# Other assumed DMA durations in the build-time planner of a two-layer transformer kernel, and the program order that follows from them

## The chip, the cores and the metric

One core of a Trainium2 chip runs the whole kernel. The metric is the device time of one execution in microseconds (us). The kernel uses all five instruction streams of the core: TensorE (PE, with its weight loads shown as PEld), VectorE (DVE), ScalarE (ACT), GpSimd (POOL) and SyncE (SP), which here only issues DMA transfers.

## The reference, cut to what matters

Two identical layers over a sequence of 2048 tokens with 512 features; attention has 32 heads of 16 features, the feed-forward part 1792 hidden features. All arrays are bf16.

```python
def A(x, wqkv, wo):                      # attention
    q, k, v = heads(x @ wqkv)            # 32 heads, Dh = 16
    p = softmax(q @ k^T * Dh ** -0.5)    # 2048 x 2048 per head
    return heads_back(p @ v) @ wo
def B(x, w1, b1, w2, b2):                # feed-forward
    return gelu(x @ w1 + b1) @ w2 + b2
for layer in range(2):
    x = x + A(layernorm(x), wqkv, wo)
    x = x + B(layernorm(x), w1, b1, w2, b2)
```

## The kernel before

**Tiling.** The 2048 queries of a layer are cut into four segments of 512 (the very last one into two of 256). A pass takes one segment and four heads (eight passes a segment, line 1109), and walks over 16 key tiles of 128. A cell is one head, one key tile and 512 queries: its scores are one matmul (L1244), which three cells share side by side, and their exponentials fill 512 columns of PSUM for each cell. Most cells go to ACT, two or three to an instruction (L1601, `0.065 + 0.4267 * n` in the planner's units); the others go to DVE and POOL, which make the exponential by integer arithmetic on the bits (L1396 from PSUM, then L1473 on POOL and L1478 on DVE). The product with V (L1665) gathers a pass in one PSUM bank, and `norm` (L805) divides by the sum.

**What runs beneath it.** Attention of one segment runs while PE also does the rest of the layer for the segment before it: the output projection `wo` (L861), a layer norm, the first feed-forward matmul `hpair` (L948), gelu on ACT (L982), the second matmul `ytile` (L1001), the next layer norm and the next layer's projections (L777). All their matmuls are recorded at L556, in steps of eight matmuls, four of which stand side by side in the PE array.

**Weights.** Feed-forward and projection weights don't stay on the core. `wloads` (L891) streams them as pieces of 256 KB into a ring of four buffers `wr`, each load issued by SP at L933 when the matmuls that used the buffer before are done. Each tile of `ytile` alone takes seven such pieces. For the last half segment four pieces go to a part of `kt` instead (`wlate`, L937); all four write under the same keys (`over`), so each of them waits for the one before it to land.

**Layer norm.** DVE takes the statistics, POOL scales a 128-token tile into one of two buffers `xln` (L689), and SP issues a DMA transpose of it into `xf`, `xp` or `kt` (L693). Only the first four tiles and the last two are transposed by PE instead (L700).

**Who sets the order.** Nothing is written in order by hand. Each part above is a Python generator that yields operations (`_Op`, L186) with an engine, an assumed duration `cost`, and, for a DMA, an assumed `tail` from the end of its issue to its landing. `_Sched.run` (L362) keeps a clock for each engine, picks the operation that can start first by its own arithmetic (with priorities among those that are ready), and appends it to that engine's program. The end that others wait for is set in one line:

```python
self.end[ev] = start + cost + op.tail + LATENCY[e]          # L420
```

The semaphore waits come from the true data dependencies (`_Prog`, L84), so the order is free of races whatever is assumed; what the assumed durations change is only where each instruction stands in its engine's program. Each engine runs its program strictly in order. Where PE would be free for a while by the plan, `fill` (L340) puts matmuls without a use into its program (L1232). Feed-forward steps are also held back to set fractions of the attention's progress (`when`, L1038, with the tables `HB`, `HS`, `YB`, `YS`, `PACE`).

The lines that the change touches: `LATENCY` (L212), the moves of `x` between HBM and the core (`xmove`, L621), the DMA transpose (L693), the weight load (L933) and the store of the output (L1034).

Of the kernel before, what the change touches and what calls it, by code (L numbers as in the profile page):

```python
# [28 lines left out]
XT = 8  # L29
# [179 lines left out]

OWN = 0.022  # L210
HEAD = 0.14
LATENCY = {"pe": 0.219, "act": 0.21, "dve": 0.139, "pool": 0.153328, "sp": 0.1}  # L212
OVERLAP = 0.083
ROUND = 1.02

# [1 line left out]
class _Sched:  # L217
# [122 lines left out]
    def fill(self, start, nxt):  # L340
        while self.filler and self.mode:
# [17 lines left out]
            self.clock["pe"] = now + into + MM + cold  # L359
            self.end[ev] = self.clock["pe"] + LATENCY["pe"]  # L360

    def run(self):  # L362
        while True:
# [55 lines left out]
            self.clock[e] = start + cost  # L419
            self.end[ev] = start + cost + op.tail + LATENCY[e]  # L420
            for x in op.after:
# [4 lines left out]
                self.clock[e] = at + MM  # L426
                self.end[ev] = at + MM + LATENCY[e]
            if e == "dve" and op.port:
# [117 lines left out]
class _Plan:  # L546
# [72 lines left out]
        yield ("give", "loaded")  # L619

    def xmove(self, c, src, dst, sem, reads, writes):  # L621
        yield _Op("sp", 0.42, lambda e: e.dma_start(dst, src), reads=reads, writes=writes, sem=sem, by=16, tail=3.7)

    def xfeed(self, h):
        keys = ["X.%d" % (t % XT) for t in range(4 * h, 4 * h + 4)]
# [58 lines left out]
    def ln_tile(self, c, t, dst, dkeys, quick):  # L684
        T = self.T
        ph = self.phase[t // 4]
        x = yield ("acq", "xln")
        eng, cost = ("dve", 0.4) if quick else ("pool", 0.77)
        yield _Op(eng, cost, lambda e: e.tensor_scalar(  # L689
            T["XLN"][:, x, :], T["X"][:, t % XT, :], T["RSTD"][:, t:t + 1], T["NMR"][:, t:t + 1], op0=ALU.mult, op1=ALU.add),  # L690
            reads=["X.%d" % (t % XT), "RSTD.%d" % c, "NMR.%d" % c], writes=["XLN.%d" % x])
        if not quick:
            yield _Op("sp", 1.2, lambda e: e.dma_start(dst(t), T["XLN"][:, x, :], transpose=True),  # L693
                      reads=["XLN.%d" % x], writes=dkeys(t), sem="dtr%d" % x, by=16, tail=1.35)
            yield ("rel", "xln", x)
            yield ("give", ("lnt", t, ph))
            return
        b = yield ("acq", "misc")
        tb = self.bank(b).bitcast(BF16)
        fns = [lambda e, dc=dc: e.transpose(tb[:, dc * 128:(dc + 1) * 128], T["XLN"][:, x, dc * 128:(dc + 1) * 128],  # L700
                                            T["IDENT"][:, :]) for dc in range(NDC)]
        yield _Op("pe", 4 * TR, fns, reads=["XLN.%d" % x, "IDENT"], writes=["B.%d" % b], prio=0.8)
        yield ("rel", "xln", x)
        t3 = tb[:, 0:512].rearrange("p (c q) -> p c q", c=NDC)
        if ph == 0 or t % 2 == 0:
            yield _Op("act", DV, lambda e: e.copy(dst(t), t3), reads=["B.%d" % b], writes=dkeys(t))
        else:
            yield _Op("dve", DV, lambda e: e.tensor_copy(dst(t), t3), reads=["B.%d" % b], writes=dkeys(t))
        yield ("rel", "misc", b)
        yield ("give", ("lnt", t, ph))  # L710
# [219 lines left out]

    def wload(self, piece, src, n, uses, w, over):
        dst = self.T["WR"][w].rearrange("p (c f) -> p c f", c=n)
        yield _Op("sp", 0.37, lambda e: e.dma_start(dst, src), writes=["WR.%d" % w] + over, sem="dwr%d" % w, by=16, tail=2.48)  # L933
        self.wleft[piece] = uses
        yield ("give", ("w",) + piece, w)

# [64 lines left out]
    def ytile(self, l, seg, t):  # L1001
        T = self.T
        tail = l == NL - 1 and seg[0] == self.NQ - 1
        last = NFC // 2 - 1
        for p in range(1 if tail else NFC // 2):
            yield ("need", ("g", l, seg, p))
        b = None if tail else (yield ("need", ("w", l, seg, "2", (t, 0))))
        b = yield ("acq", "misc")
        pb = self.bank(b)
        q = slice((t % 4) * 128, (t % 4) * 128 + 128)  # L1010
        for p in range(NFC // 2):
            yield ("need", ("g", l, seg, p))
            if tail and p < last:
                yield ("need", ("w2", p // 2))
                wk, ws = "W2.%d" % (p // 2), [T["Q"][:, f % 4, 512 * (f // 4):512 * (f // 4) + 512] for f in (2 * p, 2 * p + 1)]
            else:
                piece = (NL - 1, self.segs[NL - 1][-1], "2", last) if tail else (l, seg, "2", (t, p))
                w = yield ("need", ("w",) + piece)
                wk, ws = "WR.%d" % w, [T["WR"][w][:, 512 * j:512 * j + 512] for j in range(2)]
            fns = []  # L1020
            for j in range(2):
                fns += self.quads(pb, T["G"][:, 2 * p + j, q], ws[j], p + j == 0, False)
            if p == last:
                fns += self.quads(pb, T["ONES1"][:, :], T["B2row"][:, :], False, True)
            yield _Op("pe", len(fns) // 4 * MM, fns, reads=[wk, "ONES1", "B2row"] + ["G.%d.%d" % (f, t % 4) for f in (2 * p, 2 * p + 1)],
                      writes=["B.%d" % b], prio=MID if p else FPRIO, mode="P")
            if not tail or p == last:
                yield from self.wdone(piece, w)
        yield _Op("dve", DV, lambda e: e.tensor_tensor(out=T["X"][:, t % XT, :], in0=T["X"][:, t % XT, :], in1=pb, op=ALU.add),
                  reads=["B.%d" % b, "X.%d" % (t % XT)], writes=["X.%d" % (t % XT)])  # L1030
        yield ("rel", "misc", b)
        yield ("give", ("xready", t, 2 * l + 2))
        if l == NL - 1:
            yield _Op("sp", 0.42, lambda e: e.dma_start(self.hbm["out"][:, t, :], T["X"][:, t % XT, :]), reads=["X.%d" % (t % XT)],  # L1034
                      writes=["OUT.%d" % t], sem="dout", by=16, tail=2.0)
            yield ("give", ("xout", t))

# [735 lines left out]
```

## Time and profile before

| | |
|---|---|
| median of three runs | 1532.86 us (1531.32 to 1536.05) |
| the profiled execution | 1531.3 us |
| its span, first to last instruction | 1529.5 us |
| busy: PE, DVE, ACT, POOL | 1441.2, 1335.0, 1477.3, 821.9 us |
| mean granted TensorE clock | 0.999 |
| DMA traffic | 103.40 MB, 68 GB/s on the mean |

The span leaves out 1.8 us of the profiled execution's own time (1531.3 less 1529.5). The profiled execution lies 1.6 us below the median. "Idle before" in the views below is the time in which an engine stood still ahead of an instruction, with what ended it; matmuls overlap each other, so their durations can't be added.

### The profile page before, as it was taken

The numbers are of one execution on the slowest core, as the hardware profiler recorded it, in microseconds if no ns is written. First come the engines' busy times: TensorE is split into PE (matmuls) and PEld (weight loads), VectorE is DVE, ScalarE is ACT, GpSimd is POOL, SyncE is SP. The second block draws the span as 40 slices with busy tenths as digits, with TensorE's granted clock in tenths as the row PEclk, the third lists the DMA queues.
The fourth block names the chain that finished last, engine by engine and source line by source line (L and its number), as shares of the span: only waits on it lengthen the run. The fifth ranks groups of instructions, "written<-read, shape, count | busy, mean of one in ns | idle before, by whom it ended". The sixth has DMA issues, their size and how long they took to land.

```text
span 1529.5 us, 46372 instructions
## 1 busy us (share of the span) xinstructions
PE 1441.2 (94%) x20257; PEld 441.6 (29%) x20257; DVE 1335.0 (87%) x2259; ACT 1477.3 (97%) x1369; POOL 821.9 (54%) x785
## 2 busy tenths in 40 slices
PE   8998899999999999999999999899999999999998
PEld 3222222222222222222222222222222222334345
DVE  6568889989998999978799778899989989999994
ACT  7999999999999999999999999999999999999995
POOL 5435546655564755545465455567555646464550
PEclk9999999999999999999999999999999999999999
DMA  5100001052111521126121441001143105311523
GB/s 155 41 2 1 2 12 40 29 174 77 48 31 53 144 83 36 43 64 166 50 56 38 130 133 29 1 2 36 37 151 93 43 23 170 109 36 33 167 69 98
DMA packets 145046, 103.40 MB, mean 68 GB/s; under 512 B 37069, under 2 KB 143822, under 8 KB 144846
## 3 DMA queue, kind: packets, MB, share of 16 engines
q1 hardware_dynamic: 144846, 100.44, 23.2%
q8 instruction: 162, 2.65, 0.7%
q14 instruction: 38, 0.31, 0.1%
HBM read 88.61 MB, written 4.19 MB: 61 GB/s over the span
## 4 chain that ended last, share of the span: by engine, by line
ACT 40%; PE 39%; DVE 14%; DMA 5%; POOL 1%; issue 1%; SPq 0%; DVEq 0%; ACTq 0%; POOLq 0%
ACT pt L1601 32%; PE ps L556 13%; PE ps L1665 13%; PE ps L1244 12%; DVE du L1396 6%; DVE du L1478 4%; DMA wr<-in_B_w_dram 2%; ACT kt L1601 2%; ACT q L1601 2%; ACT g L997 2%; DVE g L976 1%; ACT v L1601 1%; POOL xln L689 1%; DMA kt<-in_B_w_dram 1%; DMA xp<-xln 1%
## 5 line engine op out<-in xcount | busy, mean ns | idle before, releaser
L1601 ACT ACTIVATE pt<-ps 128x1024 bf16<-128x1024 f32 (+1 forms) x1112 | 1198.2, 1218 | 19.1 <-PE ps L1244 13.3
L1473 POOL TENSOR_SCALAR du<-du 128x1024 uint16<-128x1024 uint16 (+1 forms) x479 | 562.2, 1175 | 495.6 <-DVE du L1396 481.2
L1396 DVE TENSOR_SCALAR du<-ps 128x512 uint16<-128x512 f32 x956 | 634.9, 680 | 93.5 <-PE ps L1244 88.6
L1244 PE MATMUL ps<-qp,kt 32*128 32x512 bf16 x4096 | 530.0, 384 | 37.3 <-ACT pt L1601 20.7
L1665 PE MATMUL ps<-pt,v 128*17 128x512 bf16 (+1 forms) x2876 | 407.3, 360 | 11.4 <-ACT pt L1601 6.3
L1665 PE MATMUL ps<-du,vc 128*17 128x512 bf16 (+1 forms) x3228 | 384.3, 357 | 3.5 <-ACT pt L1601 1.8
L1478 DVE TENSOR_SCALAR du<-du 128x2048 uint16<-128x2048 uint16 (+1 forms) x479 | 351.4, 743 | 10.7 <-POOL du L1473 10.6
L1244 PEld LDWEIGHTS ps<-qp,kt 32*128 32x128 bf16 x4096 | 137.2, 91 | 581.6 <-ACT pt L1601 214.1
L1665 PE MATMUL ps<-du,v 128*17 128x512 bf16 (+1 forms) x1076 | 178.7, 358 | 10.3 <-ACT pt L1601 3.3
L1673 PE MATMUL ps<-vc,zero 128*17 128x512 bf16 x919 | 182.5, 381 | 0.0
L556 PE MATMUL ps<-xf,wr 128*32 128x512 bf16 (+1 forms) x1888 | 129.5, 364 | 4.2 <-DMA xf<-xln 2.0
L1665 PEld LDWEIGHTS ps<-pt,v 128*17 128x17 bf16 x2876 | 99.2, 88 | 108.0 <-issue 65.2
L1665 PEld LDWEIGHTS ps<-du,vc 128*17 128x17 bf16 x3228 | 100.2, 89 | 89.5 <-issue 54.8
L556 PE MATMUL ps<-wr,g 128*32 128x512 bf16 x1600 | 117.6, 384 | 7.6 <-DMA wr<-in_B_w_dram 6.4
L1192 POOL TENSOR_SCALAR qp<-q,mask 128x512 bf16<-128x512 bf16 (+1 forms) x91 | 71.1, 781 | 76.6 <-PE ps L1244 69.9
L1601 ACT ACTIVATE kt<-ps 128x1536 bf16<-128x1536 f32 (+1 forms) x77 | 98.9, 1294 | 2.9 <-PE ps L1244 1.2
L976 DVE TENSOR_SCALAR g<-ps,hb1t 128x512 bf16<-128x512 f32 (+1 forms) x112 | 78.4, 703 | 6.0 <-PE ps L556 5.4
L1473 POOL TENSOR_SCALAR kt<-kt 128x1024 uint16<-128x1024 uint16 (+1 forms) x46 | 53.4, 1161 | 46.9 <-DVE kt L1396 46.8
L1601 ACT ACTIVATE v<-ps 128x1024 bf16<-128x1024 f32 (+1 forms) x69 | 73.9, 1139 | 2.0 <-PE ps L1244 1.2
L1396 DVE TENSOR_SCALAR kt<-ps 128x512 uint16<-128x512 f32 x91 | 62.0, 681 | 7.3 <-PE ps L1244 5.6
L1665 PE MATMUL ps<-kt,v 128*17 128x512 bf16 (+1 forms) x309 | 67.5, 365 | 0.3 <-ACT pt L1601 0.2
L1665 PEld LDWEIGHTS ps<-du,v 128*17 128x17 bf16 x1076 | 45.1, 88 | 63.3 <-issue 25.7
(90 smaller groups left out, 1234.0 us busy)
## 6 DMA issues: line engine op xcount, KB each, us to landing
wr<-in_B_w_dram SPq DMA_DIRECT2D x256, 256.0 KB, 2.9
wr<-in_A_wqkv_dram SPq DMA_DIRECT2D x24, 256.0 KB, 3.0
wr<-in_A_wo_dram SPq DMA_DIRECT2D x18, 256.0 KB, 3.6
x<-in_A_x_dram SPq DMA_DIRECT2D x7, 512.0 KB, 4.1
kept<-x SPq DMA_DIRECT2D x4, 512.0 KB, 2.9
x<-kept SPq DMA_DIRECT2D x4, 512.0 KB, 3.9
out_dram<-x SPq DMA_DIRECT2D x16, 128.0 KB, 2.4
g<-in_A_wqkv_dram SPq DMA_DIRECT2D x3, 512.0 KB, 5.1
```

The costliest lines, as they stand in the source:

```text
L556: return [lambda e, a=a: e.matmul(out[32 * a:32 * a + 32, :], lhsT=lhsT[:, 32 * a:32 * a + 32], rhs=rhs, start=start, stop=stop, tile_posi ...
L689: yield _Op(eng, cost, lambda e: e.tensor_scalar(T["XLN"][:, x, :], T["X"][:, t % XT, :], T["RSTD"][:, t:t + 1], T["NMR"][:, t:t + 1], op0 ...
L976: yield _Op("dve", 0.21 + n / 966, lambda e, fc=fc, pb=pb: e.tensor_scalar(T["G"][:, fc, q], pb, T["HB1T"][:, fc:fc + 1], None, op0=ALU.ad ...
L997: lambda e, g=g: e.activation(out=g, in_=g, func=ACT.Gelu_apprx_tanh), reads=gk, writes=gk, prio=2)
L1192: yield _Op("pool", 0.27 + 0.42 * w / 512, lambda e, s=s, q=q, i=i, t=t, w=w: e.tensor_scalar(T["QP"][:, s, w * i:w * i + w], q, T["MASK"] ...
L1244: return (lambda e: e.matmul(o, lhsT=lhsT, rhs=rhs, start=True, stop=True, tile_position=(32 * a, 0)), ["K%d.%d.%d" % (l, gb, kt // 4), "Q ...
L1396: yield _Op("dve", 0.682, lambda e: e.tensor_scalar(u, self.bank(b), E_SCALE, E_BIAS, op0=ALU.mult, op1=ALU.add), reads=["B.%d" % b], writ ...
L1473: one = _Op("pool", 0.15 + 0.45 * n, lambda e, a=a, b=b: e.tensor_scalar(b, a, float(SHIFT), 1.0, op0=ALU.add, op1=ALU.mult), reads=key[0] ...
L1478: two = _Op("dve", 0.152 + 0.266 * n, lambda e: e.tensor_scalar(U[:, 2:4, 0:n, :], U[:, 0:2, 0:n, :], 2 * SHIFT, None, op0=ALU.add), reads ...
L1601: yield _Op("act", 0.065 + 0.4267 * n, lambda e, src=src, dst=dst: e.activation(out=dst, in_=src, func=ACT.Exp, scale=0.25), reads=["B.%d" ...
L1665: op.fns.append(lambda e, o=o, lhsT=q[0][0][m], rhs=q[0][1][:, n * m:n * m + n], a=a, st=st, sp=sp: e.matmul(o, lhsT=lhsT, rhs=rhs, start= ...
L1673: op.fns.append(lambda e, o=self.bank(b)[32 * a:32 * a + 17, :], rhs=rhs, a=a, st=not begun[a], sp=end: e.matmul(o, lhsT=T["ZERO"][:, 0:17 ...
```

## The change

Five entries of the planner's table take other values; no operation, buffer, dependency or priority is edited. "Issue" is the time that the plan takes on SP, "tail" the time from there to landing; with SP's 0.1 of `LATENCY` the three add up to the assumed time from issue to use.

| operation | issue + tail before | after |
|---|---|---|
| `xmove` (512 KB) | 0.42 + 3.7 | 1.5 + 4.0 |
| DMA transpose | 1.2 + 1.35 | 0.3 + 3.5 |
| weight load (256 KB) | 0.37 + 2.48 | 1.5 + 2.5 |
| output store | 0.42 + 2.0 | 1.0 + 2.0 |
| `LATENCY["pe"]` | 0.219 | 0.2175 |

```diff
-LATENCY = {"pe": 0.219, "act": 0.21, "dve": 0.139, "pool": 0.153328, "sp": 0.1}
+LATENCY = {"pe": 0.2175, "act": 0.21, "dve": 0.139, "pool": 0.153328, "sp": 0.1}
...
     def xmove(self, c, src, dst, sem, reads, writes):
-        yield _Op("sp", 0.42, lambda e: e.dma_start(dst, src), reads=reads, writes=writes, sem=sem, by=16, tail=3.7)
+        yield _Op("sp", 1.5, lambda e: e.dma_start(dst, src), reads=reads, writes=writes, sem=sem, by=16, tail=4.0)
...
-            yield _Op("sp", 1.2, lambda e: e.dma_start(dst(t), T["XLN"][:, x, :], transpose=True),
-                      reads=["XLN.%d" % x], writes=dkeys(t), sem="dtr%d" % x, by=16, tail=1.35)
+            yield _Op("sp", 0.3, lambda e: e.dma_start(dst(t), T["XLN"][:, x, :], transpose=True),
+                      reads=["XLN.%d" % x], writes=dkeys(t), sem="dtr%d" % x, by=16, tail=3.5)
...
-        yield _Op("sp", 0.37, lambda e: e.dma_start(dst, src), writes=["WR.%d" % w] + over, sem="dwr%d" % w, by=16, tail=2.48)
+        yield _Op("sp", 1.5, lambda e: e.dma_start(dst, src), writes=["WR.%d" % w] + over, sem="dwr%d" % w, by=16, tail=2.5)
...
-            yield _Op("sp", 0.42, lambda e: e.dma_start(self.hbm["out"][:, t, :], T["X"][:, t % XT, :]), reads=["X.%d" % (t % XT)],
+            yield _Op("sp", 1.0, lambda e: e.dma_start(self.hbm["out"][:, t, :], T["X"][:, t % XT, :]), reads=["X.%d" % (t % XT)],
```

Because the plan is a chain of choices, the order of all engines differs from about 28 us on. Counted in the two programs: ACT has 15 more exponentials of two cells, 9 fewer of three and 1 fewer of one; DVE's L1396 does 1045 cells where it did 1047; 53 more groups of `fill` (L1232, 212 matmuls) and 114 fewer matmuls with zero weights that pad rounds of the product with V (L1673). SP's 405 issues are the same ones in another order.

## The prediction

> **What bounds the kernel now.** I read the page's busy shares first, then ACT's work over two stretches, then what PE waited for, and last ACT's timeline, gap by gap.
>
> ```profile
> PE 1441.2 (94%) x20257; PEld 441.6 (29%) x20257; DVE 1335.0 (87%) x2259; ACT 1477.3 (97%) x1369; POOL 821.9 (54%) x785
> ```
> ```profile
> 28.55:1500.00 1471.45, 1392.46 (x19389) 416.74 (x19385) 1308.05 (x2184) 1447.33 (x1329) 806.64 (x757) 1.00 0.23 65
> 1500.00:1529.50 29.50, 25.05 (x613) 16.43 (x601) 10.84 (x27) 11.06 (x18) 1.10 (x2) 1.00 0.34 101
> ```
>
> In the stretch table the fourth figure with a count is ACT. From 28.55 to 1500 us it works 1447.33 of 1471.45 us: ACT's exponentials set the time there, and only 24.1 us of idle can be won unless its work shrinks. In the last 29.5 us ACT has little to do and PE has 25.05 us of work: that tail goes by PE and by what PE waits for. The order is the same in both programs up to about 28 us, so the head counts nothing.
>
> PE, 94% busy, runs close behind ACT. Its waits for transfers:
>
> ```profile
> PE ps L556 <- DMA wr<-in_B_w_dram: 6.4, 8, 1.1
> PE ps L556 <- DMA xp<-xln: 2.4, 3, 1.2
> PE ps L556 <- DMA xf<-xln: 2.0, 3, 1.6
> PE ps L556 <- DMA kt<-in_B_w_dram: 1.6, 1, 1.6
> PE ps L556 <- DMA wr<-in_A_wqkv_dram: 1.0, 1, 1.0
> ```
>
> The columns are total, times, longest: 13.4 us in 16 waits, 1.6 of it in the tail. Do they reach ACT? In PE's timeline the first and the last long one before the tail are these:
>
> ```profile
> 362.38 0.61 PE L556 MATMUL ps<-xp,wr 128*32 128x512 bf16 x8 [1.24 <-DMA xp<-xln]
> 1482.93 0.62 PE L556 MATMUL ps<-xf,wr 128*32 128x256 bf16 x16 [1.62 <-DMA xf<-xln]
> ```
>
> About 1 us behind each long wait ACT stands still, named as waiting for PE's score matmuls, because these queue behind the stalled step:
>
> ```profile
> 363.37 5.62 ACT L1601 ACTIVATE pt<-ps 128x1024 bf16<-128x1024 f32 x6 [0.90 <-PE ps L1244]
> 499.41 14.77 ACT L1601 ACTIVATE pt<-ps 128x1024 bf16<-128x1024 f32 x15 [0.85 <-PE ps L1244]
> 539.30 1.02 ACT L1601 ACTIVATE q<-ps 128x1024 bf16<-128x1024 f32 x1 [0.48 <-PE ps L1244]
> 687.97 1.02 ACT L1601 ACTIVATE pt<-ps 128x1024 bf16<-128x1024 f32 x1 [0.84 <-PE ps L1244]
> 689.91 1.02 ACT L1601 ACTIVATE pt<-ps 128x1024 bf16<-128x1024 f32 x1 [0.92 <-PE ps L1244]
> 691.11 3.28 ACT L1601 ACTIVATE pt<-ps 128x1024 bf16<-128x1024 f32 x3 [0.18 <-PE ps L1244]
> 757.26 2.79 ACT L1601 ACTIVATE pt<-ps 128x1536 bf16<-128x1536 f32 x2 [0.71 <-PE ps L1244]
> 866.31 2.14 ACT L1601 ACTIVATE kt<-ps 128x1024 bf16<-128x1024 f32 x2 [0.70 <-PE ps L1244]
> 888.89 4.20 ACT L1601 ACTIVATE pt<-ps 128x1024 bf16<-128x1024 f32 x4 [0.57 <-PE ps L1244]
> 904.22 128.79 ACT L1601 ACTIVATE pt<-ps 128x1024 bf16<-128x1024 f32 x110 [0.61 <-PE ps L1244]
> 1422.85 3.90 ACT L1601 ACTIVATE v<-ps 128x1024 bf16<-128x1024 f32 x4 [0.61 <-PE ps L1244]
> 1483.92 7.61 ACT L1601 ACTIVATE pt<-ps 128x1024 bf16<-128x1024 f32 x8 [1.39 <-PE ps L1244]
> ```
>
> These sum to 8.8 us (0.90+0.85+0.48+0.84+0.92+0.18+0.71+0.70+0.57+0.61+0.61+1.39). The second and third of the three near 690 follow two PE waits of 2.05 us together, and I count them as the same debt. So 8.8 of ACT's 24.1 us of idle are late transfers; 15.3 us are not.
>
> **Why they are late.** The lines below are what the transfers took, issue to landing, weight loads first, transposes second; and how long each occupies SP:
>
> ```profile
> DMA to landing us min/median/max: 2.5/3.0/5.9
> DMA to landing us min/median/max: 2.4/2.5/4.9
> ```
> ```profile
> L933 SPq DMA_DIRECT2D wr<-in_B_w_dram x256: 367/368/1429, 10.1 to 1506.8; - x128
> L693 SPq DMA_TRANSPOSE xf<-xln x30: 1188/1200/2162, 236.9 to 1478.7; - x30
> ```
>
> The plan assumed 0.37+2.48+0.1 = 2.95 us for a weight load, and half of the loads take 3.0 or longer. It assumed 2.65 us for a transpose, against 4.9 for the worst. The plan thus puts the using matmul where it is just in time for the median, and the upper half is late in a program that can't be reordered.
>
> The Trainium skill, page "DMA: Bandwidth & Descriptors", section "Anatomy of one DMA — SWDGE (gpsimd) path", gives a fit of about 2.0 us plus bytes over 436 GB/s, which for 256 KB is an estimate of 2.6 us. By it the old entries would have covered every load; the trace's 3.0 and 5.9 and its 16 waits disagree, on loads issued by SP.
>
> **The change part by part.** *Weight loads* (4.1 us assumed). I took both program orders and counted, for each of the 302 loads, PE's work between the matmul that frees the buffer (or lets an earlier SP issue go) and the first matmul that reads the load, at these prices from the chain around 743 us:
>
> ```profile
> 742.10 0.32 PE ps L1244 x3
> 744.26 0.43 PE ps L556 x8
> ```
>
> Before, the shortest distance is 1.97 us and 30 loads have 3.2 us or less; after, the shortest is 2.95 and two have 3.2 or less. Up to 3.5 us it is 38 loads before and five after. If the waits follow that count, 5/38 of the weights' 7.4 us are left, 1 us; I leave 0.8 on ACT. *Transposes* (3.9 us assumed): three of the gaps above (0.90, 0.61, 1.39) are theirs; 3.9 lies above the median of 2.5 by more than these waits, so they go. SP's part falls from 1.2 to 0.3 in the plan while the row says 1.2; four in a burst may be 0.9 us later each than planned, which the 1.4 us between 3.9 and 2.5 covers for one but not for all four: this is where a wait of the same kind can return, and the reason for the 0.8. Sum on ACT: **-8.0 us** (ends: 0 if the waits were not the cause, -8.8 if all go).
>
> *ACT's work.* 15 more exponentials of two cells, 9 fewer of three, one fewer of one:
>
> ```profile
> L1601 ACT ACTIVATE pt<-ps 128x1024 bf16<-128x1024 f32 x753 | 735.9, 1072 | 16.1 <-PE ps L1244 12.6 <-PE ps L1665 2.1
> L1601 ACT ACTIVATE pt<-ps 128x1536 bf16<-128x1536 f32 x358 | 511.6, 1526 | 3.0 <-PE ps L1665 1.4 <-PE ps L1244 0.7 <-PE ps L1673 0.6
> ```
> ```profile
> 1499.18 0.59 ACT L1601 ACTIVATE pt<-ps 128x512 bf16<-128x512 f32 x1
> ```
>
> 15 x 1.072 - 9 x 1.526 - 0.59 = **+1.8 us**, all on ACT's path (less if neighbours overlap, as busy times of a pipelined engine do). Two cells fewer on DVE and four fewer POOL and DVE steps take nothing off the path: these engines stand idle 13% and 46%.
>
> *Tail.* The chain at the end is the four serial loads into `kt` (first and last shown), then PE, then the last addition and store:
>
> ```profile
> 1501.78 4.04 DMA kt<-in_B_w_dram
> ...
> 1512.25 2.88 DMA kt<-in_B_w_dram
> 1515.18 11.49 PE ps L556 x296
> ```
>
> The fourth load costs PE the 1.6 us wait listed above. In SP's order the first `kt` load stands behind loads that need buffers of the half segment before. Before, these come free only among the 72 matmuls that PE does after the last product with V; after, all those steps stand ahead of it, the one that lets the first load go with at least six score groups still to come (six exponentials of about 1 us). The four loads are then early by more than 1.6 us. What is late next: the 72 matmuls no longer cover the last normalisation,
>
> ```profile
> 1500.93 2.15 PE L556 MATMUL ps<-xf,wr 128*32 128x256 bf16 x72
> 1501.17 0.72 DVE L834 STREAM_TRANSPOSE xt<-ps 128x512 f32<-128x512 f32 x1 [2.56 <-PE ps L1673]
> 1501.81 2.01 DVE L976 TENSOR_SCALAR g<-ps,hb1t 128x256 bf16<-128x256 f32 x5
> 1504.54 0.45 DVE L853 STREAM_TRANSPOSE otn<-ott 128x256 bf16<-128x256 bf16 x1
> ```
>
> which took from 1501.17 to 1504.99 with 1.9 us of bias additions in its middle; those move ahead too, and 1.9 us plus a short hand-over remains in which PE has nothing. The moved work and the opened gap cancel (2.0 against about 2.1). Tail: **-1.4 us** (ends -3.5 and +0.5).
>
> *Stores and moves of x.* The store's and `xmove`'s longer entries only shift SP's places; PE's waits above name none of them. I count nothing, unless a store ahead of a weight load holds it: in the new order most stores need no wait of their own. `LATENCY["pe"]`, 1.5 ns less, only tips choices.
>
> Sum: -8.0 + 1.8 - 1.4 = **-7.6 us**. The profiled execution, 1531.3, would be 1523.7; the median lies 1.6 above, so **1525.3 us**.
>
> **The rivals.**
>
> *The stalls become filler (same).* The new order has 53 more filler groups on PE, each 0.22 us (four of the 0.43 for eight). A group is free only while ACT has work queued; PE runs it even when the data is already there, since the order is fixed. For it: the plan makes gaps because it thinks data late. Against: there are 114 fewer padding matmuls, and PE's total by the same prices differs by 1 us. With half of them on the path, 53/2 x 0.22 = 5.8: 1531.1.
>
> *The new order collides on POOL and DVE (slower).* Around 787 us POOL's two `xln` steps took longer than usual, a product with V came late behind them, and ACT waited:
>
> ```profile
> L689 POOL TENSOR_SCALAR xln<-x,rstd,nmr x58: 760/775/2246, 20.5 to 1477.4; 128x512 bf16<-128x512 bf16 x58
> 791.85 6.46 ACT L1601 ACTIVATE pt<-ps 128x1024 bf16<-128x1024 f32 x6 [1.88 <-PE ps L1665]
> ```
>
> The 58 tiles are some fourteen bursts of four, each with POOL and DVE in a new order. The price is 1.88 us a burst; with nine more such bursts 1525.3 + 16.9 = 1542.2. From seven on it is slower by over 0.3%. Against: one burst in fourteen does it now, and the planner keeps the entries of POOL and DVE as they were. The Trainium skill, page "SBUF — State Buffer", section "Who interferes with whom", says DVE and GpSimd share one port pair as an exclusive lock; the row's 775 and 2246 ns agree.
>
> *The change doesn't do what it says (same).* If ACT's 8.8 us were due to plan gaps that stand there anyway, only work and tail count: 1532.9 + 1.8 - 1.4 = 1533.3. Against: the DMA waits are PE's own rows.
>
> **How the numbers follow.** Forecast 0.62 (its own range 1519 to 1528); filler 0.17 (1528.5 to 1535); no effect 0.06; collision 0.15. A measurement here tells about 0.3%, 4.6 us, from no change: faster is below 1528.3, slower above 1537.5. The 15.3 us of other idle are dealt anew by the new order: a third of it, 5 us either way, widens the forecast. The range reaches from 1518 to 1535 and leaves out the collision and the ends. Faster 0.62, same 0.23, slower 0.15.
>
> **What would show it.** Right: PE's waits for DMA fall from 13.4 us to under 3; ACT's idle between 28.55 us and the last exponential falls from 24 to 14-18 us; ACT's exponentials grow by 1 to 2 us; no wait for `kt` in the last 20 us. Wrong: the DMA waits go but ACT's idle stays near 24 (filler, or other waits of L1244); POOL's `xln` mean rises and waits on L1665 lengthen (collision); the DMA waits stay (the entries were not the cause).

## The result, and the profile after

After takes 1520.91 us (median; 1520.74 to 1524.36) where before took 1534.45 beside it: the ratio is 0.9917 [0.989, 0.9944], 13.5 us less. Beside the experiments before ran 52 times more, with a median of 1532.3; against that after gains 11.4 us. The forecast was 1525.3, 7.6 us less: the sign was right, the size too small. The two profiled executions, 1531.3 and 1524.36 us, differ by 6.9 us. They are before's shortest of the first comparison and after's longest, so they show less than the medians. A second trace of after (e8, 1518.8 us of span where the first has 1522.5) is the usual one.

The page of after, busy time and share of the span:

```profile
PE 1449.7 (95%) x20337; PEld 446.0 (29%) x20337; DVE 1333.5 (88%) x2255; ACT 1477.5 (97%) x1374; POOL 823.6 (54%) x783
```

ACT's total is that of before (1477.3). PE's waits for transfers, total, times and longest:

```profile
PE ps L556 <- DMA xf<-xln: 1.3, 1, 1.3
```

One row is left: 13.4 us have become 1.3 (13.6 with a sixth row of before that the prediction leaves out, one wait of 0.2 us of L1244 for `xp`). To see where the time went I cut each execution in two, at the start of ACT's one late table load, which follows the last exponential. The rows give from:to, length, then busy time of PE, PEld, DVE, ACT and POOL, PE's granted clock, DMA share and GB/s. Before, then after (first trace), then after (e8):

```profile
28.55:1499.79 1471.24, 1392.25 (x19381) 416.54 (x19377) 1308.05 (x2184) 1447.12 (x1329) 806.64 (x757) 1.00 0.23 65
1499.79:1529.50 29.71, 25.26 (x621) 16.62 (x609) 10.84 (x27) 11.27 (x18) 1.10 (x2) 1.00 0.34 100
```
```profile
28.11:1496.02 1467.91, 1404.34 (x19548) 423.58 (x19540) 1308.66 (x2185) 1447.34 (x1334) 808.33 (x754) 1.00 0.24 66
1496.02:1522.50 26.48, 22.51 (x526) 14.28 (x522) 8.81 (x22) 11.12 (x18) 1.06 (x2) 1.00 0.19 57
```
```profile
28.29:1492.34 1464.05, 1400.06 (x19548) 424.05 (x19540) 1308.15 (x2185) 1446.50 (x1333) 808.18 (x754) 1.00 0.24 66
1492.34:1518.80 26.46, 22.51 (x526) 14.29 (x522) 8.81 (x22) 11.12 (x18) 1.07 (x2) 1.00 0.19 58
```

In the middle ACT works as long in all three; its idle (length less ACT's busy time) is 24.12 us before, 20.57 in the first trace of after and 17.55 in the second. The tail is 29.71 before and 26.5 after, both times.

**Why the first trace of after is 3.7 us longer than the second.** Both have one late transpose at the same place. In the first, PE's timeline and ACT's behind it, start, duration, what, and in brackets the idle time ahead:

```profile
247.81 1.04 PE L556 MATMUL ps<-xf,wr 128*32 128x512 bf16 x8 [1.35 <-DMA xf<-xln]
```
```profile
249.44 1.02 ACT L1601 ACTIVATE kt<-ps 128x1024 bf16<-128x1024 f32 x1 [2.00 <-PE ps L1244]
250.95 1.02 ACT L1601 ACTIVATE kt<-ps 128x1024 bf16<-128x1024 f32 x1 [0.49 <-PE ps L1244]
252.46 1.02 ACT L1601 ACTIVATE pt<-ps 128x1024 bf16<-128x1024 f32 x1 [0.48 <-PE ps L1244]
253.97 3.02 ACT L1601 ACTIVATE pt<-ps 128x1024 bf16<-128x1024 f32 x3 [0.48 <-PE ps L1244]
```

One late transfer, four gaps, 3.45 us. The stretches around it, with the same columns as above (granted clock third from the end), show what went with it:

```profile
246.00:248.00 2.00, 0.65 (x11) 0.27 (x12) 1.39 (x3) 1.44 (x2) 1.42 (x1) 0.88 0.00 0
248.00:250.00 2.00, 2.00 (x19) 0.24 (x11) 0.56 (x1) 0.56 (x1) 0.00 (x0) 0.50 0.00 0
250.00:252.00 2.00, 2.00 (x18) 0.33 (x14) 1.48 (x3) 1.49 (x2) 1.04 (x1) 0.50 0.00 0
252.00:254.00 2.00, 2.00 (x18) 0.34 (x19) 1.32 (x3) 1.05 (x2) 0.77 (x1) 0.50 0.00 0
```

PE's granted clock falls to a half, and each step takes longer (eight matmuls 1.04 us) for as long as that lasts. In half-microsecond stretches it is a half from 247.5 to about 254.3 us, 6.8 us. In e8 the wait is 0.97 us, the clock stays at 1.00 and ACT loses 0.98 us:

```profile
246.77 0.62 PE L556 MATMUL ps<-xf,wr 128*32 128x512 bf16 x8 [0.97 <-DMA xf<-xln]
```
```profile
247.75 2.14 ACT L1601 ACTIVATE kt<-ps 128x1024 bf16<-128x1024 f32 x2 [0.98 <-PE ps L1244]
```

Before's own trace has such a stretch, near 690 us, behind two waits:

```profile
684.00:686.00 2.00, 0.94 (x11) 0.22 (x11) 0.58 (x1) 2.00 (x2) 0.00 (x0) 1.00 0.86 274
686.00:688.00 2.00, 1.52 (x19) 0.47 (x23) 0.14 (x2) 1.16 (x3) 1.05 (x1) 0.78 0.60 195
688.00:690.00 2.00, 2.00 (x19) 0.38 (x15) 1.28 (x3) 1.08 (x2) 0.00 (x0) 0.50 0.46 143
690.00:692.00 2.00, 2.00 (x26) 0.43 (x22) 1.55 (x4) 1.82 (x2) 1.05 (x1) 0.87 0.38 131
```

Here it is half from about 687.1 to 690.5, 3.4 us. I call these stretches half-clock patches. Most of the rest of the 3.7 us between the two traces of after is one more gap of ACT, 1.12 us at 217.22, behind a patch near 214 (last section).

### The profile page after: what moved, and what is told of

It reads as the page before. It is cut to its first block, busy times and chain, and to the rows that moved or that the text cites. A ratio compares the mean times of both kernels' runs of the same rounds, so it can differ in the third digit from the quotient of the medians.

```text
span 1522.5 us, 46554 instructions
## 1 busy us (share of the span) xinstructions
PE 1449.7 (95%) x20337; PEld 446.0 (29%) x20337; DVE 1333.5 (88%) x2255; ACT 1477.5 (97%) x1374; POOL 823.6 (54%) x783
## 4 chain that ended last, share of the span: by engine, by line
ACT 58%; PE 29%; DVE 10%; issue 1%; POOL 1%; DMA 0%; ACTq 0%; DVEq 0%
ACT pt L1601 47%; PE ps L556 10%; PE ps L1244 9%; PE ps L1665 9%; ACT kt L1601 4%; DVE du L1396 4%; ACT g L997 3%; ACT v L1601 2%; DVE du L1478 2%; ACT q L1601 1%; DVE kt L1396 1%; PE ps L1232 1%; DVE g L976 1%; ACT L1601 1%; ACT L997 1%
## 5 line engine op out<-in xcount | busy, mean ns | idle before, releaser
L1601 ACT ACTIVATE pt<-ps 128x1024 bf16<-128x1024 f32 (+1 forms) x1115 | 1195.5, 1213 | 13.5 <-PE ps L1244 9.2
L1473 POOL TENSOR_SCALAR du<-du 128x1024 uint16<-128x1024 uint16 x478 | 558.6, 1170 | 482.9 <-DVE du L1396 469.3
L1396 DVE TENSOR_SCALAR du<-ps 128x512 uint16<-128x512 f32 x955 | 635.6, 683 | 82.5 <-PE ps L1244 77.6
L1244 PE MATMUL ps<-qp,kt 32*128 32x512 bf16 x4096 | 532.0, 385 | 29.9 <-ACT pt L1601 18.1
L1665 PE MATMUL ps<-pt,v 128*17 128x512 bf16 (+1 forms) x2866 | 400.6, 361 | 11.5 <-ACT pt L1601 7.9
L1665 PE MATMUL ps<-du,vc 128*17 128x512 bf16 (+1 forms) x3213 | 372.9, 359 | 5.0 <-DVE du L1478 2.0
L1478 DVE TENSOR_SCALAR du<-du 128x2048 uint16<-128x2048 uint16 x478 | 350.5, 744 | 12.0 <-POOL du L1473 11.7
L1244 PEld LDWEIGHTS ps<-qp,kt 32*128 32x128 bf16 x4096 | 137.7, 91 | 570.0 <-ACT pt L1601 191.9
L1673 PE MATMUL ps<-vc,zero 128*17 128x512 bf16 x805 | 167.0, 381 | 0.0
L1192 POOL TENSOR_SCALAR qp<-q,mask 128x512 bf16<-128x512 bf16 (+1 forms) x91 | 76.1, 837 | 63.6 <-PE ps L1244 56.5
L1601 ACT ACTIVATE kt<-ps 128x1536 bf16<-128x1536 f32 (+1 forms) x81 | 102.0, 1268 | 5.0 <-PE ps L1244 3.6
L1473 POOL TENSOR_SCALAR kt<-kt 128x1024 uint16<-128x1024 uint16 x45 | 54.6, 1214 | 75.8 <-DVE kt L1396 74.2
L1601 ACT ACTIVATE v<-ps 128x1024 bf16<-128x1024 f32 (+1 forms) x74 | 85.6, 1187 | 2.7 <-PE ps L1244 1.1
L1396 DVE TENSOR_SCALAR kt<-ps 128x512 uint16<-128x512 f32 x90 | 61.6, 684 | 14.0 <-PE ps L1244 12.3
L1665 PE MATMUL ps<-kt,v 128*17 128x512 bf16 (+1 forms) x314 | 71.1, 365 | 1.4 <-DVE kt L818 0.6
```

The costliest lines, as they stand in the source:

```text
L1192: yield _Op("pool", 0.27 + 0.42 * w / 512, lambda e, s=s, q=q, i=i, t=t, w=w: e.tensor_scalar(T["QP"][:, s, w * i:w * i + w], q, T["MASK"] ...
L1244: return (lambda e: e.matmul(o, lhsT=lhsT, rhs=rhs, start=True, stop=True, tile_position=(32 * a, 0)), ["K%d.%d.%d" % (l, gb, kt // 4), "Q ...
L1396: yield _Op("dve", 0.682, lambda e: e.tensor_scalar(u, self.bank(b), E_SCALE, E_BIAS, op0=ALU.mult, op1=ALU.add), reads=["B.%d" % b], writ ...
L1473: one = _Op("pool", 0.15 + 0.45 * n, lambda e, a=a, b=b: e.tensor_scalar(b, a, float(SHIFT), 1.0, op0=ALU.add, op1=ALU.mult), reads=key[0] ...
L1478: two = _Op("dve", 0.152 + 0.266 * n, lambda e: e.tensor_scalar(U[:, 2:4, 0:n, :], U[:, 0:2, 0:n, :], 2 * SHIFT, None, op0=ALU.add), reads ...
L1601: yield _Op("act", 0.065 + 0.4267 * n, lambda e, src=src, dst=dst: e.activation(out=dst, in_=src, func=ACT.Exp, scale=0.25), reads=["B.%d" ...
```

## The experiments

The theory, *late transfers*: the time went because matmuls no longer wait for transfers that come after the plan's time. The rival, *new deal*: any edit of the table deals the whole order anew, and this order happens to be a good one. A second question is which of the durations carries it.

The "PE figure" below is `LATENCY["pe"]`. The table gives for each version the median and the ratio to before in its own comparison, then from its trace ACT's busy time and idle in the middle, how much of that idle is late, PE's waits for DMA (the tail's too), and the tail. Before's median is that of the 52 executions, its trace the one of the prediction. "Late" is ACT's gaps of 0.1 us or more that end up to 4.5 us behind a matmul that had waited for DMA, plus those in a half-clock patch, whatever wait stands ahead of the patch; it is worked out from the two timelines (before: 8.8 + 0.2; after, first: 1.1 of the 4.6 lies in the patch near 214, which follows no transfer).

| version | median us | ratio [interval] | ACT busy | idle | of it late | PE's DMA waits | tail |
|---|---|---|---|---|---|---|---|
| before | 1532.3 | 1 | 1447.1 | 24.1 | 9.0 | 13.6 | 29.7 |
| after, first | 1520.91 | 0.9917 [0.989, 0.9944] | 1447.3 | 20.6 | 4.6 | 1.3 | 26.5 |
| e1 PE figure only | 1534.92 | 1.001 [0.9995, 1.0025] | 1452.1 | 29.0 | 10.1 | 11.1 | 26.3 |
| e2 weights only | 1537.43 | 1.0027 [1.0016, 1.0037] | 1454.1 | 27.1 | 5.6 | 6.3 | 26.3 |
| e3 transposes only | 1534.87 | 1.0006 [0.9993, 1.002] | 1454.2 | 25.8 | 7.7 | 9.3 | 26.8 |
| e4 after, old PE figure | 1524.83 | 0.9947 [0.9932, 0.9961] | 1451.5 | 16.4 | 1.4 | 1.5 | 27.1 |
| e5 before, PE waits for no weight load | 1527.41 | 0.9974 [0.9958, 0.9989] | 1445.7 | 16.1 | 1.6 | 6.7 | 34.4 |
| e6 before, nor for a transpose | 1522.84 | 0.9943 [0.9924, 0.9963] | 1444.8 | 15.1 | 1.1 | 4.0 | 32.5 |
| e7 after, for neither | 1519.59 | 0.9922 [0.9901, 0.9943] | 1446.1 | 17.2 | 1.2 | 1.2 | 26.4 |
| e8 after again | 1520.87 | 0.9933 [0.9911, 0.9955] | 1446.5 | 17.6 | 1.0 | 1.0 | 26.5 |
| e9 after, old weight entry | 1523.39 | 0.9946 [0.9931, 0.9962] | 1447.7 | 18.8 | 5.2 | 7.8 | 27.0 |
| e10 after, old transpose entry | 1521.94 | 0.9941 [0.9925, 0.9956] | 1448.5 | 19.7 | 4.2 | 2.9 | 27.0 |
| e11 after, weights 1.0 more | 1529.46 | 0.9984 [0.9975, 0.9993] | 1447.3 | 18.9 | 0.9 | 0.9 | 33.2 |
| e12 after, weights 0.5 more, PE figure 0.217 | 1520.52 | 0.9928 [0.9916, 0.994] | 1446.5 | 17.9 | 0.7 | 0.5 | 26.3 |

**e1: a new deal without the durations.**

```diff
-LATENCY = {"pe": 0.219, "act": 0.21, "dve": 0.139, "pool": 0.153328, "sp": 0.1}
+LATENCY = {"pe": 0.2175, "act": 0.21, "dve": 0.139, "pool": 0.153328, "sp": 0.1}
```

> Before with PE's semaphore figure alone lowered (0.219 to 0.2175); the planner's transfer durations stay as they were. The program order is dealt anew, but the distances stay short: 28 weight loads within 3.2 us of PE's work of their first use and 43 within 3.5 (before 30 and 38, after 2 and 5), shortest transpose distance 1.8 us (before 1.6, after 2.5). Its exps come to 1376.0 us by the page's durations per form (before 1372.3, after 1373.5). Theory 'late transfers': PE's waits for DMA stay at 10 to 17 us (before 13.4, after 1.3), stretches of lowered granted clock follow them, ratio to before 1.000 to 1.005. Rival 'new deal' (any new order gains, the durations have nothing to do with it): ratio near 0.992.

It is 1.001: this new order by itself gains nothing. Its waits, total, times, longest:

```profile
PE ps L556 <- DMA wr<-in_B_w_dram: 7.7, 10, 1.5
PE ps L556 <- DMA xp<-xln: 3.0, 3, 1.2
PE ps L1244 <- DMA wr<-in_A_wqkv_dram: 0.4, 1, 0.4
```

They stay, 11.1 us. The short tail of after is there already, 26.3 us: it has nothing to do with the assumed durations. What it saves, ACT's work gives back (1452.1).

**e2: the weight loads alone.**

```diff
-        yield _Op("sp", 0.37, lambda e: e.dma_start(dst, src), writes=["WR.%d" % w] + over, sem="dwr%d" % w, by=16, tail=2.48)
+        yield _Op("sp", 1.5, lambda e: e.dma_start(dst, src), writes=["WR.%d" % w] + over, sem="dwr%d" % w, by=16, tail=2.5)
```

> Before with the weight loads' duration alone raised (1.5 + 2.5 in place of 0.37 + 2.48). Weight loads: 3 within 3.2 us of PE's work, 8 within 3.5, shortest 3.05. Transposes stay short (shortest 1.7). Exps 1378.3 us, 6.0 more than before by count. Theory 'late transfers': PE's waits on the weight tile are gone (of 13.4 us), those on xf stay, 2 to 6 us; idle of ACT some 5 to 8 us less, exps 6 more: ratio 0.995 to 1.000. Rival 'the transposes carry it': waits of PE for DMA above 8 us, ratio 1.00 or above. Rival 'new deal': 0.992.

```profile
PE ps L556 <- DMA xf<-xln: 5.4, 6, 1.1
PE ps L556 <- DMA xp<-xln: 0.9, 1, 0.9
```

The waits on the weight tile are gone, as expected, and late idle falls from 9.0 to 5.6; yet the time is 1.0027, above what I expected. ACT works 7.0 us more, and the idle that is not late is 21.5 us where before has 15.1. The largest single gap waits for PE's products with V and has no DMA wait ahead of it:

```profile
1055.99 4.62 ACT L1601 ACTIVATE pt<-ps 128x1536 bf16<-128x1536 f32 x4 [4.45 <-PE ps L1665]
```

**e3: the transposes alone.**

```diff
-            yield _Op("sp", 1.2, lambda e: e.dma_start(dst(t), T["XLN"][:, x, :], transpose=True),
-                      reads=["XLN.%d" % x], writes=dkeys(t), sem="dtr%d" % x, by=16, tail=1.35)
+            yield _Op("sp", 0.3, lambda e: e.dma_start(dst(t), T["XLN"][:, x, :], transpose=True),
+                      reads=["XLN.%d" % x], writes=dkeys(t), sem="dtr%d" % x, by=16, tail=3.5)
```

> Before with the transposes' duration alone changed (0.3 + 3.5 in place of 1.2 + 1.35). Transposes: shortest distance 2.5 us; weight loads stay short: 28 within 3.2 us, 36 within 3.5, shortest 1.97. Exps 1378.9 us, 6.6 more than before by count. Theory 'late transfers': PE's waits on xf go, those on the weight tile stay, 7 to 12 us, with stretches of lowered clock behind them; ratio 1.000 to 1.005. Rival 'the transposes carry it': waits below 4 us and a ratio of 0.993 to 0.997. Rival 'new deal': 0.992.

```profile
PE ps L556 <- DMA wr<-in_B_w_dram: 7.9, 13, 1.2
PE ps L556 <- DMA xf<-xln: 1.1, 1, 1.1
PE ps L556 <- DMA wr<-in_A_wqkv_dram: 0.3, 1, 0.3
```

The mirror image: the transposes' waits are down to one, the weights' stay. 1.0006 is what late transfers expected, and ACT's work is 7.1 us longer here too.

**e4: all durations of after, the old figure for PE.**

```diff
-LATENCY = {"pe": 0.2175, "act": 0.21, "dve": 0.139, "pool": 0.153328, "sp": 0.1}
+LATENCY = {"pe": 0.219, "act": 0.21, "dve": 0.139, "pool": 0.153328, "sp": 0.1}
```

> After with PE's semaphore figure set back to 0.219; all four transfer durations as in after. The order is dealt anew, the distances stay long: 3 weight loads within 3.2 us, 7 within 3.5, shortest 2.83; shortest transpose 2.6. Exps 1377.0 us, 3.5 more than after. Theory 'late transfers': PE's waits for DMA stay below 3 us, ratio to before 0.991 to 0.995. Rival 'new deal': the gain belongs to the one order that 0.2175 dealt, ratio 0.998 to 1.003.

0.9947: another order, ACT's work 5 us longer than in after, and still 8.7 us below before, with 1.5 us of DMA waits and no half-clock patch in the middle of its trace. With e1 this speaks against new deal, but from e1 to e4 each comparison still mixes two things, so the next three keep the order.

**e5, e6, e7: the same order, without the waits.** On PE, ACT, DVE and POOL the program is that of before (e5, e6) or after (e7), instruction for instruction. The key lines, first for the loads and then for the transposes (`real` is true for the first into each tile; the waits of PE on a transpose are capped there in the same way):

```diff
-            need[sem] = max(need.get(sem, 0), val)
+            need[sem] = max(need.get(sem, 0), 16 if eng == "pe" and sem in ("dwr0", "dwr1", "dwr2", "dwr3") else val)
...
-        dst = self.T["WR"][w].rearrange("p (c f) -> p c f", c=n)
+        dst = (self.hbm["sink"][:, w, :] if w < W_RING and self.P.cnt["dwr%d" % w] else self.T["WR"][w]).rearrange("p (c f) -> p c f", c=n)
```
```diff
-            yield _Op("sp", 1.2, lambda e: e.dma_start(dst(t), T["XLN"][:, x, :], transpose=True),
+            yield _Op("sp", 1.2, lambda e: e.dma_start(dst(t), T["XLN"][:, x, :], transpose=True) if real else e.dma_start(self.hbm["sink"][:, x, 0:512], T["XLN"][:, x, :]),
```

> Before, with every instruction of PE, ACT, DVE and POOL in its old order, but no matmul waits for a weight load: each of the four slots keeps the first weights that were loaded into it, and the later loads, issued at the same places of SP's queue behind the same releases, go to a scratch tensor in memory (left out: the later weights, so the output is that of the first ones). Theory 'late transfers': the order is that of before, and yet PE's waits on the weight tile (7.4 of 13.4 us) and the lowered clock behind them are gone; the waits on xf and xp stay: ratio to before 0.994 to 0.997. Rival 'new deal' (the order gained, not the transfers): ratio 1.000.

> The one before this, and in the same way no matmul waits for a transpose into xf or xp after the first into each tile: the normalised rows are copied to the scratch tensor (left out: the later transposes too). Order of before on all four engines. Theory 'late transfers': PE waits for no DMA in the middle but the tail's; the 8.8 us of ACT's gaps behind them and the patches of lowered clock go: 1533.5 to 1522 to 1525, ratio 0.992 to 0.995; mean granted clock 1.0 in nearly all runs, and so a narrower spread than before's 12 us. Rival 'new deal': 1.000. If the ratio falls short of after's 0.991, what is left is the tail (3.2 us).

> The same edit made to after: order of after on all four engines, no matmul waits for a weight load or a transpose (the later weights and transposes left out). Theory 'late transfers': after waits for one transfer only, so nothing is left to gain but that one: ratio to before 0.989 to 0.992, at most 2 us below after. Rival (late transfers cost both orders alike, and the gain of after lies elsewhere): the ratio falls by as much as before's does, to 0.984 to 0.987.

In its own comparison before takes 1531.5; free of the weight loads' waits it takes 1527.4, free of both 1522.8. With no instruction of a compute engine moved, 8.7 us go. What e6 still waits for is the last load into `kt`, in the tail, and the first transposes into `xp` and `xf`, which it keeps:

```profile
PE ps L556 <- DMA kt<-in_B_w_dram: 2.5, 1, 2.5
PE ps L556 <- DMA xp<-xln: 1.3, 1, 1.3
PE ps L556 <- DMA xf<-xln: 0.2, 1, 0.2
```

After loses only 1.3 us by the same edit (1520.87 to 1519.59): it had almost nothing left to wait for, and whatever else the edit changes (where the loads land, copies in place of transposes) is worth no more than that there. For the middle this settles it for late transfers; the tail is another matter (see the next part). The two stretches of e6:

```profile
28.24:1488.06 1459.82, 1390.45 (x19381) 417.33 (x19377) 1307.31 (x2184) 1444.75 (x1328) 805.22 (x757) 1.00 0.22 66
1488.06:1520.60 32.54, 27.06 (x621) 17.54 (x609) 10.84 (x27) 11.70 (x18) 1.10 (x2) 0.95 0.31 91
```

The middle is 11.4 us shorter than before's, with the same instructions. The tail is 2.8 us longer; PE waits 2.5 us there for the last load into `kt` and has a half-clock patch (0.95). e5's tail is 4.7 us longer for the same two reasons (waits 3.7, clock 0.90). So the medians show less than the middle gains. The spread goes as well: e6 lies between 1522.43 and 1523.67, before beside it between 1528.83 and 1537.27.

**e8: after once more.**

> After, unchanged, a second time for another trace and for the chip that the three runs before use. Ratio 0.989 to 0.994. 'Late transfers': most runs show a granted clock of 1.0 and lie within 0.5 us of each other; a run with a lower mean clock is 2 to 4 us longer. The trace of such a usual run has no stretch of lowered clock, and ACT's idle in the middle is 16 to 17 us where the first trace had 20.6.

The median comes back (1520.87), the clock is 1.00 all through the middle, and idle is 17.55 us, a little above the 16 to 17 expected.

**e9 and e10: after with one duration set back.** The edits are those of e2 and e3 reversed, made to after.

> After with the weight loads' old duration (0.37 + 2.48), the rest as in after; the order is dealt anew. Weight loads are short again: 28 within 3.2 us of PE's work, 32 within 3.5, shortest 1.97; transposes long (2.6). Exps 1373.4 us by count, as in after (1373.5). Theory 'late transfers': PE's waits on the weight tile are back, 5 to 8 us, lowered clock in some runs, median 1525 to 1529 (ratio to before 0.994 to 0.997). Rival (the transposes carry the gain): within 2 us of after, 1520 to 1523.

> After with the transposes' old duration (1.2 + 1.35), the rest as in after; dealt anew. Shortest transpose 2.0 us (after 2.5, before 1.6), weight loads 4 within 3.2 and 7 within 3.5. Exps 1373.5 us by count, as in after. Theory 'late transfers': PE waits 2 to 5 us on xf and xp, none or little on the weight tile; median 1521 to 1525. Rival (the transposes carry the gain): 1526 to 1530.

e9's waits on the weight tile are back, and not on much else:

```profile
PE ps L556 <- DMA wr<-in_B_w_dram: 6.7, 10, 1.0
PE ps L556 <- DMA xf<-xln: 1.1, 1, 1.1
```

But the time is 1523.39, less than I expected, and close to the rival's range. Late idle is 4.2 us more than in e8 (5.2 against 1.0); the rest of the idle is 13.6 against 16.6, so the new order gave back 2.9. Against before, e9 keeps a gain of 8.5 us in its own comparison with 7.8 us of DMA waits still there; of the 7.6 us between the two spans, 3.8 are late idle, 2.7 the tail and 1.5 the other idle. Late transfers are thus only half of this version's gain. e10 is as expected, 1521.94, with 2.9 us of waits. Neither duration carries the gain alone; the weights' share is the larger, by late idle (5.2 and 4.2, and in the fixed order 9.5 of the 11.4 us of the middle went with the weights; by the medians, with e5's longer tail, 4.1 of 8.7).

**e11 and e12: longer still.**

```diff
-        yield _Op("sp", 1.5, lambda e: e.dma_start(dst, src), writes=["WR.%d" % w] + over, sem="dwr%d" % w, by=16, tail=2.5)
+        yield _Op("sp", 1.5, lambda e: e.dma_start(dst, src), writes=["WR.%d" % w] + over, sem="dwr%d" % w, by=16, tail=3.5)
```
```diff
-LATENCY = {"pe": 0.2175, "act": 0.21, "dve": 0.139, "pool": 0.153328, "sp": 0.1}
+LATENCY = {"pe": 0.21700, "act": 0.21, "dve": 0.139, "pool": 0.153328, "sp": 0.1}
...
-        yield _Op("sp", 1.5, lambda e: e.dma_start(dst, src), writes=["WR.%d" % w] + over, sem="dwr%d" % w, by=16, tail=2.5)
+        yield _Op("sp", 1.5, lambda e: e.dma_start(dst, src), writes=["WR.%d" % w] + over, sem="dwr%d" % w, by=16, tail=3.00)
```

> After with the weight loads' duration a microsecond longer still (1.5 + 3.5): no load stands within 3.5 us of its use, shortest 3.60. Exps 1371.8 us by count (after 1373.5), fill groups 347 (after 325). Theory 'late transfers': after had almost nothing left to wait for, so the longer distance gives nothing by itself and the time follows ACT's work: 1518 to 1522. Rival (longer is always better, or a load that comes too early holds something up): below 1516 or above 1525.

> After with the weight loads' duration 1.5 + 3.0 and PE's semaphore figure 0.217: chosen from the program orders alone, for long distances (shortest load 3.05, 1 within 3.2, 4 within 3.5; shortest transpose 2.5) and little work of ACT (1371.3 us by count, after 1373.5, before 1372.3) with few fill groups (284; after 325, before 272). Theory: time is ACT's work plus late transfers plus gaps of the deal: PE's waits for DMA below 2 us, median 1516 to 1520. If ACT's work is not what orders the versions without late transfers, 1521 or more.

e11 is 1529.46, as its rival said, and 6.75 of the 8.6 us that it loses to after (e8) are in the tail:

```profile
1494.29:1527.50 33.21, 29.07 (x688) 19.02 (x688) 10.88 (x28) 11.45 (x18) 1.06 (x2) 1.00 0.34 97
```
```profile
1494.77 2.80 PE L556 MATMUL ps<-xf,wr 128*32 128x256 bf16 x96
```

PE has 688 matmuls there where after has 526; 96 of them are the feed-forward of the half segment before, which after does ahead of its last exponential. The first load into `kt` goes out 3.7 us behind the late table load here (at 1498.0), in e8 9.7 us ahead of it (at 1482.6). That work has slipped past the point where ACT's work hides it. Whether the longer duration did this is not shown: it is one order, and before, with the shortest durations, has such a tail too (29.7 us, first `kt` load at 1501.8). The middle is within the range of the others. e12 takes 1520.52, a hair above the 1516 to 1520 that I expected and level with after: the 2.2 us less of exponentials that I had counted don't show (ACT busy 1446.5 in both). No version here beats after by more than a measurement tells.

## Why the prediction was right, and where its sizes were off

The spans are 1529.5 for before and 1518.8 for after (e8), 10.7 us. With e6 between them they split, against the forecast's terms, so:

| step of the prediction | forecast | measured, and from which rows |
|---|---|---|
| late transfers on ACT | -8.0 | -11.4 (middle 1471.24 to 1459.82, e6, same order) |
| ACT's work | +1.8 | +1.75 (busy 1444.75 in e6, 1446.50 in e8) |
| idle dealt anew | 0, "5 us either way" | +2.5 (15.07 in e6, 17.55 in e8) |
| tail | -1.4 | -3.25 (29.71 to 26.46) |
| head | 0 | -0.26 (28.55 to 28.29) |

*Weight loads and transposes: right in mechanism, mis-sized.* Of 8.8 us of gaps I let 8.0 go; idle fell by 9.05 (24.12 to 15.07). What I did not count is ACT's busy time, which fell by 2.4 us with the same steps. Part of it can be read in the rows: six exponentials back to back took 5.62 us, 0.92 for each and 1.02 for the last, so each that stands alone costs 0.10 more, and twelve gaps 1.2 us. The other 1.2 us stay open. The Trainium skill, page "ScalarE: Activation LUTs", section "What ACT_TABLE_LOAD costs", gives an overlap of about 93 ns for activations back to back; the 0.10 us of these rows agree. "I count them as the same debt", of the second and third gap near 690, was wrong as a reading: the one ends inside a half-clock patch (687.1 to 690.5) and the other just behind it.

*From profile to median: this step failed.* I added 1.6 us to the profiled execution, as if before and after had the same scatter. They don't. Before's 52 executions by their mean granted clock:

| mean clock | executions | mean time us |
|---|---|---|
| 1.000 | 11 | 1530.7 |
| 0.999 | 23 | 1532.1 |
| 0.998 | 12 | 1534.6 |
| 0.997 | 5 | 1535.5 |
| 0.994 | 1 | 1540.6 |

About 1.6 us for each thousandth; a patch of 3.4 us at half clock takes 1.7 us of clock, 0.0011 of the span. Before's profiled execution has one patch; by that figure a third of the 52 (18, those at 0.998 and below) have two or more. This is an estimate, and the slope need not be the clock's alone: the waits ahead of a patch cost ACT time too. Of after's eight executions five are at 1.000, between 1520.6 and 1521.0. So where the two spans differ by 10.7 us the medians differ by 11.4 (the 52) to 13.5 (the first comparison).

*ACT's work: right*, once both are compared without late transfers.

*Tail: right sign, and the cancellation failed.* The wait for `kt` went, as forecast. "The moved work and the opened gap cancel (2.0 against about 2.1)" did not hold: PE's work in the tail fell by 2.75 us (25.26 to 22.51), and the wait for the last normalisation that opened is only 1.13:

```profile
1498.88 1.05 PE L556 MATMUL ps<-wr,otn 128*32 128x512 bf16 x16 [1.13 <-DVE otn L853]
```

What the short tails share is the early first `kt` load that the prediction read off the new order: it is issued 9.7 us ahead of the late table load in e8 and 2.0 us behind it in before. But the term is not owed to the longer entries as such. e1, which has none of them, has the short tail too, with that load 13 us ahead; e2 and e3 also have it (13 and 17).

*The rivals.* *Stalls become filler*: after has 53 more groups than before, but it is at most part of the 2.5 us of idle, not the 5.8 forecast for it; e12, with 284 groups where after has 325, is level with it. *Collision*: its old gap of 1.88 us stands in e6 as in before (there at 786.15), so it belongs to that order; after has no middle gap above 1.25 us but those behind the one late transfer. The sign that the prediction gave for it did not come: POOL's `xln` step takes 923 ns on the mean, before 945; that the long ones of these steps come from a shared port is not shown by any run. *Doesn't do what it says* fell with the waits: e6 shows that ACT's gaps went with them.

*What would show it*: waits below 3 us, yes (1.3 and 1.0); idle 14 to 18, yes in e8 (17.55) and no in the first trace (20.57, of it 4.6 late or in patches); exponentials 1 to 2 us more, yes against e6, though the totals on the two pages are equal; no wait for `kt`, yes.

What stays open is why e1 to e3 drew 5 to 7 us more work for ACT than before (e4 4.4), and more idle that is not late: 18.1 to 21.5 us there, 14.0 to 15.1 in before's order (before, e5, e6), 13.6 to 18.0 in after and all its variants. A table that is half long and half short does not explain it: e9 and e10 have one too, and are 8.5 and 10.0 us faster than before. Two entries were never set alone, `xmove` and the output store. They are old in e1, e2 and e3, none of which gains, and new in after, e4, e9, e10 and e12, all of which do (and in e11, which gains 2.4 us). PE's waits name neither, but what these two do to the order is not separated here from chance. So the fixed order of e5 to e7 shows that late transfers cost the order of before 8.7 us by the medians and 11.4 us in the middle; which entries it takes to get an order that has few of them and doesn't give the gain back elsewhere is not shown.

## What to carry to other kernels

In a program that can't be reordered at run time, plan a transfer with a duration from the upper end of its distribution: here a late one cost PE's wait, ACT's gap and sometimes a half-clock patch on top. Once the waits are gone, more caution has nothing left to win: half a microsecond more, with another PE figure, gave nothing (e12), and a whole one came with an order that was 8.6 us longer (e11). When an edit deals a whole order anew, hold the order and take the wait away, as in e6, before you credit the edit; two of the parts alone gave 1.0027 and 1.0006, and all five entries together 0.9917.

## What was not expected of the hardware

PE's granted clock falls to a half in a program in which PE is 94 to 95% busy, after waits of about 1 us (0.94 and 1.11 in before, 1.35 in after), for 3.4 us (before, at 687) or 6.8 us (after, at 247.5). The Trainium skill, page "TensorE: Matmul & The Clock Gate", section "Part 1: The HAM clock gate (the "warmup" mystery)", tells of a free-running activity window of about 3.4 us: the two lengths agree with one and two of these. By its table the clock falls after an idle window; here a wait of 1.35 us in one busy stretch was enough (PE works 2.4 of the 3.5 us ahead of 247.5), and one of 0.97 at the same place was not. Nor is a late transfer needed: in the first trace of after the clock is also half around 214 us, behind a wait for DVE, and ACT then stands still for 1.12 us at 217.22:

```profile
213.46 0.60 PE L1665 MATMUL ps<-du,v 128*17 128x512 bf16 x2 [0.85 <-DVE du L1396]
```

In e8 the same wait at the same place leaves the clock at 1.00:

```profile
213.62 0.39 PE L1665 MATMUL ps<-du,v 128*17 128x512 bf16 x2 [0.85 <-DVE du L1396]
```

So the length of the wait alone doesn't decide. What does is not settled by these traces.
